# Turning decayed keys into rows of 2 KB for their way through DRAM, in a linear-attention and feed-forward kernel

## The chip, the cores and the metric

The kernel runs on one core of a Trainium2 chip. The core has TensorE (matmuls and weight loads), VectorE, ScalarE, GpSimd and SyncE, which issues most transfers, and 16 DMA engines that all queues share. The metric is the device time of one execution in microseconds; the median of several executions counts. Each engine runs its own instructions in program order, and waits on semaphores for the others.

## What is computed

Two blocks, one after the other. The first is a gated linear attention with 4 batches, 8 heads, 768 positions and head size 48; the second is a feed-forward layer of 3072 tokens, 384 to 2048 to 384, with a hard-swish between.

```python
state = np.zeros((B, H, D, D))
for t in range(S):
    state = alpha[:, :, t, :, None] * state + np.einsum('bhd,bhe->bhde', k[:, :, t], v[:, :, t])
    y[:, :, t] = np.einsum('bhd,bhde->bhe', q[:, :, t], state)
# ... (B,H,S,D) -> (B*S, H*D)
h = x @ w_in
g = h * np.clip(h + 3.0, 0.0, 6.0) / 6.0
out = g @ w_out
```

The kernel works on 24 chunks of 128 positions (6 for each batch), two chunks to a group of the feed-forward layer. In a chunk, keys and queries are scaled by running products of alpha, so that scores within the chunk are a masked matmul, and the state is carried from chunk to chunk by an update "decayed keys times values". The weights come as 64-bit floats, which the kernel rounds to 32 bits with bit operations on three engines as they arrive. From group 2 on, the feed-forward layer uses sums of blocks to save matmuls.

## The kernel before

A scheduler's freedom is switched off: the program is a list of short steps in a string, each of which calls one of these functions. The steps that matter here: `la`, `lk`, `lq`, `lv` load alpha, keys, queries and values of a chunk; `w` loads a slice of the weights, and `d1` to `d4` and `dx` round it; `z` are matmuls on an identity that keep TensorE warm; `k`, `q` scale keys and queries, `sc` are the scores, `yi` and `yx` the outputs from within and across the chunk, `u` the update of the state; `fa`, `fb`, `f` and `b` are the feed-forward layer of groups 0 and 1; `M`, `P` its products from group 2 on.

Scaled keys lie with head dimensions on the partitions (`K_t`: 128 partitions hold two heads, 64 rows each with 48 used; `NP` = 4 such pairs; 128 positions). The update needs them with positions on the partitions. For chunks 0 to 5 TensorE transposes them. From chunk 6 on VectorE turns them in blocks of 32 by 32 (`kt`), SyncE writes them to DRAM (`kw`) and reads them back so that the blocks stand in their places (`kr`). The last chunk of each batch needs no update.

```python
BLK = 32
V = C // BLK            # 4
FIRST = 6
# ...
def by_blocks(to, name, j):                  # line 292: a, k and q on their way in
    nc.vector.transpose(out=to.rearrange("r p (u v) -> r p v u", v=V),
                        in_=quads[name, j % NQ][:, :, :, 0:BLK])
# ...

    def k_in_blocks(j):
        return quads["k", j % NQ].rearrange("r p v d -> r (p v d)")[:, 0 : NP * C]

    def turn_k(j):
        to = k_in_blocks(j).rearrange("r (v p c) -> r p v c", v=V, p=NP)
        nc.vector.transpose(out=to, in_=K_t[j].rearrange("r p (v s) -> r p v s", v=V))

    def write_k(j):
        far_t[j] = far.tile([BLK, V, NP, V, BLK], FP, tag="far", name="far")
        src = k_in_blocks(j).rearrange("r (v p c) -> r (v p) c", v=V, p=NP)
        to = far_t[j].rearrange("s v p o c -> o s (v p) c")
        for o in range(V):
            nc.sync.dma_start(out=to[o], in_=src[BLK * o : BLK * (o + 1)])

    def read_k(j):
        kb_t[j] = wk.tile([C, NP, C], FP, tag="kb", name="kb")
        nc.sync.dma_start(out=kb_t[j].rearrange("s p r -> s (p r)"),
                          in_=far_t.pop(j).rearrange("s v p o c -> v s (p o c)"))
# ...
    def update(j):
        if last(j):
            return
        u = bank("u", j).rearrange("r p n -> r (p n)")[:, 0 : NP * 2 * D].rearrange(
            "r (p n) -> r p n", p=NP)
        ps_t["u", j] = u
        vs = v_t[j]
        for p in range(NP):
            for a in range(2):
                nc.tensor.matmul(u[64 * a : 64 * a + D, p, D * a : D * a + D],
                                 kb_t[j][:, p, 64 * a : 64 * a + D],
                                 vs[:, 2 * p + a, (64 - D) * a : (64 - D) * a + D],
                                 start=True, stop=True)
```

Each update is eight matmuls of which two (`a` = 0 and 1) write different halves of the partitions of one PSUM bank.

The other lines named in the text: 471 and 482 are the first matmul of the feed-forward layer in groups 0 and 1 (482 for half a group), 509 their second; 592 and 692 are the first and second product from group 2 on; 288 the transposes on TensorE; 346 the scores; 440 and 450 the outputs within and across the chunk; 524 the warming matmuls.

Of the kernel before, what the change touches and what calls it, by code (L numbers as in the profile page):

```python
# [8 lines left out]
FP = mybir.dt.float32  # L9
# [8 lines left out]
def kernel(  # L18
# [32 lines left out]
    nc = tc.nc  # L51
    B, H, S, D = q.shape
# [322 lines left out]
    def k_in_blocks(j):  # L375
        return quads["k", j % NQ].rearrange("r p v d -> r (p v d)")[:, 0 : NP * C]

    def turn_k(j):
        to = k_in_blocks(j).rearrange("r (v p c) -> r p v c", v=V, p=NP)
        nc.vector.transpose(out=to, in_=K_t[j].rearrange("r p (v s) -> r p v s", v=V))  # L380

    def write_k(j):
        far_t[j] = far.tile([BLK, V, NP, V, BLK], FP, tag="far", name="far")
        src = k_in_blocks(j).rearrange("r (v p c) -> r (v p) c", v=V, p=NP)
        to = far_t[j].rearrange("s v p o c -> o s (v p) c")
        for o in range(V):
            nc.sync.dma_start(out=to[o], in_=src[BLK * o : BLK * (o + 1)])

    def read_k(j):
        kb_t[j] = wk.tile([C, NP, C], FP, tag="kb", name="kb")  # L390
        nc.sync.dma_start(out=kb_t[j].rearrange("s p r -> s (p r)"),
                          in_=far_t.pop(j).rearrange("s v p o c -> v s (p o c)"))
# [8 lines left out]
    def update(j):  # L401
# [6 lines left out]
        for p in range(NP):  # L408
            for a in range(2):
                nc.tensor.matmul(u[64 * a : 64 * a + D, p, D * a : D * a + D],  # L410
                                 kb_t[j][:, p, 64 * a : 64 * a + D],
                                 vs[:, 2 * p + a, (64 - D) * a : (64 - D) * a + D],
                                 start=True, stop=True)
# [323 lines left out]
    with tc.manual_schedule():  # L737
        run("""la.0 z.3.5 lq.0 lk.0 lk.1 ta.0 la.1 ca.0 tq.0 r.0 lv.0.0 tk.0 lq.2 p.0 tk.1 z.0.2
            la.2 k.0 ta.1 q.0 z.0.1 lq.1 ca.1 sc.0 r.1 la.3 tq.2 z.0.5 m.0 lv.3.1 k.1 w.1 ta.2
            p.1 tq.1 ca.2 kb.0 r.2 ck.0 ta.3 u.0 ca.3 z.0.2 q.1 sm.0 sc.1 lv.1.2 p.2 la.4 kb.1  # L740
            m.1 st.1 z.0.4 ck.1 lk.2 d2.1 r.3 yi.0 w.3 d1.1 z.0.4 d3.1 cy.0 dx.1 ta.4 yi.1 q.2
            p.3 tk.2 yx.1 lk.3 k.2 d4.1 cy.1 u.1 lv.2.0 sc.2 sm.1 w.0 st.2 fa.1.0 d2.3 m.2 d1.3
            kb.2 d3.3 fb.1 ck.2 u.2 lq.3 fr.0.1 yi.2 d4.3 sm.2 w.4 fg.0.1 tk.3 st.3 f.0.3.1 k.3
            d2.0 d1.0 d3.0 ca.4 tq.3 dx.0 lq.4 r.4 yx.2 z.0.5 la.5 q.3 cy.2 d4.0 fr.0.3 sc.3
            lk.5 fg.0.3 d2.4 kb.3 m.3 w.2 d1.4 fa.0.2 dx.4 d3.4 yi.3 p.4 tk.5 yx.3 d4.4 w.5 fb.0
            cy.3 tq.4 fr.0.0 f.1.4.3 q.4 d2.2 fg.0.0 d1.2 d3.2 lq.5 dx.2 f.1.3.0 w.6 fr.1.4 d4.2
            d2.5 fg.1.4 ta.5 fa.4.1 fr.1.3 d3.5 ca.5 d1.5 w.7 f.1.2.2 r.5 fa.2.3 d2.6 fg.1.3
            d4.5 k.5 d1.6 fb.4 d3.6 w.8 f.0.5.0 fr.0.4 fr.1.2 fg.0.4 d4.6 d2.7 fg.1.2 d1.7
            f.1.5.1 d3.7 fr.0.5 w.9 fb.2 p.5 fr.1.5 d2.8 fg.1.5 d4.7 tq.5 d1.8 f.0.6.2 fg.0.5
            lk.4 q.5 fr.0.2 d3.8 w.10 ck.3 f.1.7.1 fr.0.6 fg.0.2 d2.9 d4.8 fg.0.6 d1.9 lv.4.2  # L750
            d3.9 f.0.7.0 fr.1.7 w.11 fg.1.7 d4.9 tk.4 d2.10 u.3 k.4 fr.0.7 sc.5 d3.10 d1.10
            f.1.0.3 w.12 fg.0.7 d4.10 sm.3 b.0.0.2 m.5 d2.11 st.4 fr.1.0 lv.5.0 d3.11 d1.11 w.13
            sc.4 fg.1.0 b.1.0.1 d4.11 d2.12 m.4 d1.12 d3.12 w.14 kb.4 yi.5 ck.4 d4.12 u.4
            f.1.1.0 sm.4 d2.13 st.5 d1.13 w.15 d3.13 yx.5 fr.1.1 yi.4 cy.5 fg.1.1 d2.14 f.1.6.3
            d4.13 d1.14 lk.6 d3.14 yx.4 fr.1.6 la.6 b.1.1 cy.4 fg.1.6 d4.14 d2.15 d1.15 lq.6
            d3.15 b.0.1 xc.2.1 la.7 tk.6 d4.15 b.1.2 ca.6 x.0 b.0.2 y.1 y.5 y.6 y.2 b.1.3 y.3
            y.7 y.4 y.8 y.9 b.0.3 bo.1 y.10 so.1 y.11 y.15 y.13 P.1.1.0 bo.0 s.1.0.0 so.0
            s.1.1.1 s.1.2.2 s.1.3.3 M.2.15.3 s.1.4 P.1.0.1 x.1 y.16 P.1.3.2 x.2 K.1.0 y.0 x.3
            P.1.2 K.1.2 y.17 y.12 M.2.16 y.19 K.1.1 y.18 P.1.4 y.20 y.21 xc.2.3 y.23 xc.2.4
            G.1.0 xc.2.5 O.1.0 G.1.1 M.2.0.0 xc.2.6 O.1.1 s.1.5 P.1.6 r.6 xc.2.0 k.6 P.1.5  # L760
            xc.2.7 G.1.3 kt.6 O.1.3 xc.2.8 kw.6 tq.6 xc.2.9 y.14 M.2.7.1 n.2.0.8 xc.2.2 y.22
            M.2.1 p.6 n.2.7.9 M.2.8 lv.6.1 n.2.1.10 o.2.4.0 M.2.2 q.6 e.2.4 y.24 sc.6 n.2.2.11
            xc.2.10 G.1.2 ca.7 kr.6 O.1.2 M.2.3 m.6 lk.7 M.2.18.2 M.2.4 r.7 n.2.18.12 M.2.17
            n.2.4.13 lq.7 h.2.4 M.2.19 o.2.0.0 p.7 u.6 e.2.0 M.2.9 lq.8 h.2.0 M.2.5 tk.7 yi.6
            o.2.1.0 n.2.5.14 k.7 lk.8 e.2.1 M.2.10 tq.7 cy.6 M.2.6.0 n.2.10.15 h.2.1 M.2.11 q.7
            lv.7.0 kt.7 sc.7 n.2.11.9 sm.6 kw.7 o.2.6.0 M.2.12 m.7 st.7 n.2.12.13 o.2.7.0 M.2.13
            o.2.3.0 la.8 yi.7 o.2.5.0 n.2.13.11 o.2.3.1 e.2.5 M.2.14 o.2.2.0 e.2.3 h.2.5 yx.7
            h.2.3 kr.7 P.2.0.2 cy.7 o.2.2.1 la.9 o.2.6.1 e.2.2 o.2.7.1 e.2.6 h.2.2 M.3.15.0
            h.2.6 e.2.7 xc.3.1 P.2.1.1 K.2.0 s.2.0.12 h.2.7 s.2.2.13 s.2.1.11 xc.3.3 u.7
            s.2.3.15 P.2.3.3 s.2.4 xc.3.4 tk.8 xc.3.5 G.2.0 P.2.2 xc.3.6 K.2.2 s.2.5 O.2.0  # L770
            xc.3.0 xc.3.8 xc.3.7 tq.8 M.3.0.1 K.2.1 xc.3.9 ca.8 P.2.4 n.3.0.14 xc.3.2 r.8
            xc.3.10 M.3.1 k.8 G.2.1 M.3.16 kt.8 O.2.1 n.3.1.10 p.8 kw.8 P.2.6 ca.9 q.8 r.9 M.3.2
            G.2.3 lk.9 O.2.3 M.3.7.2 sm.7 n.3.2.8 sc.8 p.9 n.3.7.9 lq.9 M.3.3 o.3.4.0 st.8 m.8
            e.3.4 M.3.8 M.3.4 h.3.4 kr.8 P.2.5 tk.9 n.3.4.11 lv.8.2 o.3.0.0 lv.9.1 k.9 e.3.0
            kt.9 la.10 M.3.9 tq.9 M.3.5 o.3.1.0 u.8 G.2.2 n.3.5.12 q.9 lk.10 M.3.18.3 O.2.2 sm.8
            e.3.1 M.3.10 h.3.0 n.3.18.13 h.3.1 M.3.6.1 n.3.10.15 kw.9 o.3.6.0 M.3.19 ca.10 st.9
            M.3.11 o.3.5.0 M.3.17 r.10 e.3.5 n.3.11.9 sc.9 lq.10 h.3.5 o.3.7.0 M.3.12 m.9 yi.8
            n.3.12.11 o.3.7.1 kr.9 M.3.13 o.3.3.0 e.3.7 la.11 yi.9 tk.10 n.3.13.8 o.3.2.0 M.3.14
            o.3.3.1 yx.9 o.3.2.1 e.3.3 h.3.7 yx.8 cy.9 h.3.3 P.3.0.3 e.3.2 s.3.1.15 cy.8 h.3.2
            s.3.3.13 o.3.6.1 P.3.1.0 xc.4.1 K.3.0 k.10 e.3.6 xc.4.3 kt.10 h.3.6 kw.10 xc.4.4 u.9  # L780
            s.3.0.11 M.4.15.1 xc.4.5 s.3.2.8 s.3.4 M.4.0.2 P.3.2 xc.4.6 n.4.0.9 lv.10.0 p.10
            lk.11 G.3.0 s.3.5 O.3.0 M.4.1 K.3.1 xc.4.0 xc.4.8 xc.4.7 P.3.4 lq.11 tq.10 n.4.1.12
# [119 lines left out]
```

## Time and profile before

| | |
|---|---|
| time, median of 3 (range) | 567.42 us (565.51 to 567.97) |
| span of the profiled execution | 564.6 us, granted TensorE clock 0.994 |
| DMA packets | 121272, 53.73 MB; 80638 of them under 512 B |
| transfers of keys to DRAM | 60 of 64 KB |
| transfers of keys back | 15 of 256 KB |
| keys turned on VectorE | 15, mean 706 ns |
| state updates | 20 blocks of 16 TensorE instructions, 11.4 us busy in all |

An fp32 matmul shows as two instructions on TensorE (PE), each with its weight load (PEld), which overlaps the matmul before it; so busy time of TensorE says that something was in the pipe, not that it ran at its best rate. The chain of waits follows the execution back from its last instruction, at each step to what released it. A group is all instructions of one line, engine and operation; "mean ns of one" is from the start of an instruction to its reported end, which for VectorE lies some 80 to 160 ns after the next one has begun. A name such as `far<-kq` is a transfer or operation that writes `far` and reads `kq`; `quads["k", ...]` is called `kq`, the far tile in DRAM `far`, the keys by position `kb`.

### The profile page before, as it was taken

Reading aid. Unit: us, or ns where it says so; the run is one execution under the profiler, and the core shown is the slowest. Engines: PE = TensorE matmul, PEld = TensorE weight load, DVE = VectorE, ACT = ScalarE, POOL = GpSimd, SP = SyncE. Lnnn points to the kernel's source line nnn. Section 1 sums busy time; section 2 is a strip of 40 time slices with the busy share of each in tenths; the row PEclk is TensorE's granted clock in tenths of the full one; section 3 lists DMA queues with packets and bytes.
Section 4 is the critical chain, followed back from the end, with each engine's and each line's share of the span. In section 5 each row is a group of like instructions: output and inputs, shape, how many; then the busy total and the mean of one; then the engine's idle time right before and its main releaser. Section 6 shows DMA issues by size and latency. Waiting matters only on the chain.

```text
span 564.6 us, 12762 instructions
## 1 busy us (share of the span) xinstructions
PE 553.4 (98%) x5236; PEld 513.2 (91%) x5236; DVE 470.0 (83%) x798; ACT 196.4 (35%) x348; POOL 56.0 (10%) x70
## 2 busy tenths in 40 slices
PE   8899999999899999999999999999999999999997
PEld 7688987599799989999999999999999999999997
DVE  7866997999899999998998978976999967754580
ACT  1457664112332332322422422432521422432420
POOL 2333435200001000100000000000000000000000
PEclk9979999999999999999999999999999999999999
DMA  9999677103533636264264353153154340000000
GB/s 147 188 186 168 186 230 196 52 16 63 139 90 87 145 71 155 54 139 90 60 148 107 77 121 85 20 146 78 45 129 94 83 122 8 1 22 8 1 30 21
DMA packets 121272, 53.73 MB, mean 95 GB/s; under 512 B 80638, under 2 KB 114174, under 8 KB 121214
## 3 DMA queue, kind: packets, MB, share of 16 engines
q1 hardware_dynamic: 114588, 48.19, 40.8%
q10 hardware_dynamic: 6624, 4.72, 2.5%
q8 instruction: 41, 0.67, 0.5%
q14 instruction: 19, 0.14, 0.1%
HBM read 44.24 MB, written 8.65 MB: 94 GB/s over the span
## 4 chain that ended last, share of the span: by engine, by line
PE 89%; DMA 6%; DVE 2%; SPq 1%; issue 0%; ACT 0%; DVEq 0%; ACTq 0%
PE m_ps L692 35%; PE m_ps L592 29%; PE m_ps L471 6%; PE sc_ps L346 4%; PE m_ps L509 4%; PE y_ps L440 4%; DMA rings<-in_k_dram 3%; PE y_ps L450 2%; PE m_ps L482 2%; DMA t<-in_v_dram 2%; PE u_ps L410 2%; DMA kb<-far 1%; PE tk_ps L288 1%; DMA far<-kq 1%; PE m_ps L524 0%
## 5 line engine op out<-in xcount | busy, mean ns | idle before, releaser
L692 PE MATMUL m_ps<-w,g_sb 128*128 128x192 f32 x704 | 121.2, 328 | 0.0
L692 PEld LDWEIGHTS m_ps<-w,g_sb 128*128 128x128 f32 x704 | 113.8, 190 | 2.3 <-issue 1.4
L598 ACT COPY g_sb<-m_ps 128x512 f32<-128x512 f32 x110 | 64.3, 584 | 138.3 <-PE m_ps L592 123.9
L692 PE MATMUL m_ps<-rings,g_sb 128*128 128x192 f32 x528 | 91.2, 326 | 0.0
L692 PEld LDWEIGHTS m_ps<-rings,g_sb 128*128 128x128 f32 x528 | 85.7, 190 | 0.0
L592 PE MATMUL m_ps<-xc,w 128*128 128x128 f32 x640 | 83.2, 278 | 0.2 <-ACT g_sb L598 0.2
L592 PEld LDWEIGHTS m_ps<-xc,w 128*128 128x128 f32 x640 | 77.2, 192 | 3.3 <-issue 1.4
L487 ACT ACTIVATE r<-g_sb,half 128x512 f32<-128x512 f32 x80 | 55.5, 719 | 57.0 <-DVE g_sb L529 22.8
L491 DVE SCALAR_TENSOR_TENSOR g_sb<-r,g_sb 128x512 f32<-128x512 f32 x80 | 54.5, 700 | 8.1 <-PE m_ps L692 4.8
L397 POOL TENSOR_TENSOR t<-t,R 128x384 f32<-128x384 f32 x20 | 20.9, 1043 | 383.8 <-DVE t L425 206.0
L592 PE MATMUL m_ps<-xT,raw 128*128 128x128 f32 x400 | 51.8, 276 | 0.0
L592 PEld LDWEIGHTS m_ps<-xT,raw 128*128 128x128 f32 x400 | 48.7, 192 | 0.3
L529 DVE TENSOR_TENSOR g_sb<-m_ps,g_sb 128x512 f32<-128x512 f32 x30 | 20.5, 686 | 27.2 <-ACT g_sb L598 26.5
L592 PE MATMUL m_ps<-xT,w 128*128 128x128 f32 x320 | 41.9, 278 | 0.0
L639 DVE TENSOR_TENSOR g_sb<-g_sb 128x512 f32<-128x512 f32 (+1 forms) x55 | 41.7, 796 | 0.1
L592 PEld LDWEIGHTS m_ps<-xT,w 128*128 128x128 f32 x320 | 38.2, 192 | 1.2 <-issue 0.2
L352 DVE TENSOR_TENSOR A<-sc_ps,mask 128x512 f32<-128x512 f32 x48 | 30.8, 683 | 2.7 <-PE sc_ps L346 2.4
L592 PE MATMUL m_ps<-xc,raw 128*128 128x128 f32 x240 | 32.1, 277 | 0.7 <-ACT g_sb L598 0.7
L471 PE MATMUL m_ps<-xT,w 128*128 128x256 f32 x144 | 32.7, 381 | 0.0
L315 DVE TENSOR_TENSOR_SCAN R<-t,ones 128x516 f32<-128x516 f32 x24 | 29.3, 1223 | 3.1 <-ACT t L306 2.8
L529 DVE TENSOR_TENSOR g_sb<-g_sb 128x512 f32<-128x512 f32 x40 | 27.2, 683 | 5.5 <-ACT g_sb L598 5.4
L592 PEld LDWEIGHTS m_ps<-xc,raw 128*128 128x128 f32 x240 | 29.9, 192 | 1.2 <-ACT g_sb L598 0.9
(110 smaller groups left out, 711.4 us busy)
## 6 DMA issues: line engine op xcount, KB each, us to landing
raw<-in_moe_w_out_dram SPq DMA_DIRECT2D x8, 768.0 KB
t<-in_v_dram SPq DMA_DIRECT2D x48, 96.0 KB
raw<-in_moe_w_in_dram SPq DMA_DIRECT2D x24, 192.0 KB
out_dram<-oh ACTq DMA_DIRECT2D x44, 96.0 KB
far<-kq SPq DMA_DIRECT2D x60, 64.0 KB
kb<-far SPq DMA_DIRECT2D x15, 256.0 KB
kq<-in_k_dram SPq DMA_DIRECT2D x36, 96.0 KB
aq<-in_alpha_dram SPq DMA_DIRECT2D x36, 96.0 KB
```

The lines of the kernel that those rows point to most:

```text
L315: nc.vector.tensor_tensor_scan(out=reverse(R, n - 1, n), data0=reverse(ax, n, n), data1=reverse(ones, n, n), initial=0.0, op0=ALU.mult, op ...
L346: nc.tensor.matmul(sc[h % 2][:, h // 2], K_t[j][r, h // 2], Q_t[j][r, h // 2], start=True, stop=True)
L352: nc.vector.tensor_tensor(out=A_t[j][:, NP * o : NP * (o + 1)], in0=ps_t.pop(("sc%d" % o, j)), in1=mask.unsqueeze(1).to_broadcast([C, NP, ...
L440: nc.tensor.matmul(y_of(j, (i + 1) // 2, p), vs[:, 2 * p + a, 32 * e : 32 * e + 32], A[:, NP * a + p], start=(i % 3 == 0), stop=(i > 1 and ...
L471: nc.tensor.matmul(h[:, f], w1[:, kk, o : o + C], xT_t[g][:, kk], start=(kk == 0), stop=(kk == KT - 1))
L487: nc.scalar.activation(out=to, in_=h, func=AF.Relu, bias=half, scale=1.0 / 6.0)
L491: nc.vector.scalar_tensor_tensor(out=to, in0=r, scalar=1.0, in1=h, op0=ALU.min, op1=ALU.mult)
L529: eng.tensor_tensor(out=out, in0=in0, in1=in1, op=ALU.add if s1 > 0 else ALU.subtract)
L592: nc.tensor.matmul(acc[g][i][:, f * C : (f + 1) * C], spots[w][:, f * C : (f + 1) * C], x_of(g, x), start=(first and f == 0), stop=last, s ...
L598: nc.scalar.copy(out=slots[z], in_=acc[g][i])
L639: nc.vector.tensor_tensor(out=out, in0=in0, in1=in1, op=ALU.subtract)
L692: nc.tensor.matmul(to[g], a, rhs[:, f], start=(first and f == 0), stop=(last and f == HF - 1), skip_group_check=True)
```

## The change

The turned keys are laid out so that the four pairs `p` are innermost: a row of the turned tile is now 512 neighbouring elements (2 KB) that go to DRAM as they lie, in one transfer of 128 rows. The way back becomes four transfers, one for each block of 32 positions, each of 32 partitions by four runs of 128 elements (512 B). In place of that, VectorE's transpose writes every fourth element, and the update reads its stationary operand with a step of four elements; it takes 64 columns instead of 48, the 16 more being rows of padding whose results nobody reads. The purpose is a shorter way for the keys through DRAM: fewer small packets, and a read that doesn't have four as its slowest dimension.

```diff
--- before.py
+++ after.py
@@ -376,20 +376,26 @@
         return quads["k", j % NQ].rearrange("r p v d -> r (p v d)")[:, 0 : NP * C]
 
     def turn_k(j):
-        to = k_in_blocks(j).rearrange("r (v p c) -> r p v c", v=V, p=NP)
+        to = k_in_blocks(j).rearrange("r (v c p) -> r p v c", v=V, p=NP)
         nc.vector.transpose(out=to, in_=K_t[j].rearrange("r p (v s) -> r p v s", v=V))
 
     def write_k(j):
-        far_t[j] = far.tile([BLK, V, NP, V, BLK], FP, tag="far", name="far")
-        src = k_in_blocks(j).rearrange("r (v p c) -> r (v p) c", v=V, p=NP)
-        to = far_t[j].rearrange("s v p o c -> o s (v p) c")
-        for o in range(V):
-            nc.sync.dma_start(out=to[o], in_=src[BLK * o : BLK * (o + 1)])
+        far_t[j] = far.tile([C, NP * C], FP, tag="far", name="far")
+        nc.sync.dma_start(out=far_t[j], in_=k_in_blocks(j))
 
     def read_k(j):
         kb_t[j] = wk.tile([C, NP, C], FP, tag="kb", name="kb")
-        nc.sync.dma_start(out=kb_t[j].rearrange("s p r -> s (p r)"),
-                          in_=far_t.pop(j).rearrange("s v p o c -> v s (p o c)"))
+        to = kb_t[j].rearrange("s p r -> s (p r)").rearrange("s (o w) -> s o w", o=V)
+        src = far_t.pop(j).rearrange("(o s) (v w) -> v s o w", s=BLK, v=V)
+        for n in range(V):
+            nc.sync.dma_start(out=to[BLK * n : BLK * (n + 1)], in_=src[n])
+
+    def k_of(j, p, a):
+
+        if j < FAR:
+            return kb_t[j][:, p, 64 * a : 64 * a + D]
+        t = kb_t[j].rearrange("s p r -> s (p r)").rearrange("s (a m p) -> s a p m", a=2, p=NP)
+        return t[:, a, p]
 
     def decayed_state(j):
 
@@ -407,8 +413,8 @@
         vs = v_t[j]
         for p in range(NP):
             for a in range(2):
-                nc.tensor.matmul(u[64 * a : 64 * a + D, p, D * a : D * a + D],
-                                 kb_t[j][:, p, 64 * a : 64 * a + D],
+                n = D if j < FAR else 64
+                nc.tensor.matmul(u[64 * a : 64 * a + n, p, D * a : D * a + D], k_of(j, p, a),
                                  vs[:, 2 * p + a, (64 - D) * a : (64 - D) * a + D],
                                  start=True, stop=True)
```

The list of steps is new as well, from the first to the last word (1649 words for 1650; the same steps, but that 29 warming matmuls stand for 28). Of both lists, the start; then, of the new one, the stretch of chunk 6:

```diff
-        run("""la.0 z.3.5 lq.0 lk.0 lk.1 ta.0 la.1 ca.0 tq.0 r.0 lv.0.0 tk.0 lq.2 p.0 tk.1 z.0.2
-            la.2 k.0 ta.1 q.0 z.0.1 lq.1 ca.1 sc.0 r.1 la.3 tq.2 z.0.5 m.0 lv.3.1 k.1 w.1 ta.2
-            p.1 tq.1 ca.2 kb.0 r.2 ck.0 ta.3 u.0 ca.3 z.0.2 q.1 sm.0 sc.1 lv.1.2 p.2 la.4 kb.1
-            m.1 st.1 z.0.4 ck.1 lk.2 d2.1 r.3 yi.0 w.3 d1.1 z.0.4 d3.1 cy.0 dx.1 ta.4 yi.1 q.2
-            p.3 tk.2 yx.1 lk.3 k.2 d4.1 cy.1 u.1 lv.2.0 sc.2 sm.1 w.0 st.2 fa.1.0 d2.3 m.2 d1.3
# ...
+        run("""lk.1 z.3.5 la.0 lk.0 la.1 tk.1 lq.0 ta.0 lv.1.0 ca.0 tk.0 r.0 la.2 ta.1 z.0.2 ca.1
+            la.3 k.0 tq.0 p.0 z.0.8 lv.0.1 r.1 lq.1 ta.2 q.0 z.0.2 ca.2 w.0 k.1 sc.0 p.1 ta.3
+            m.0 kb.0 ca.3 ck.0 tq.1 r.3 yi.0 lq.3 u.0 q.1 cy.0 w.1 p.3 sc.1 sm.0 d2.0 kb.1 m.1
+            z.0.2 st.1 ck.1 tq.3 d1.0 d3.0 u.1 lq.2 yi.1 dx.0 r.2 lk.2 yx.1 q.3 d4.0 z.1.8 cy.1
+            w.4 sm.1 d1.1 d2.1 p.2 tq.2 fa.0.0 dx.1 d3.1 tk.2 lk.3 fb.0 q.2 st.2 k.2 d4.1 lv.2.2
# ...
+            P.1.6 y.19 y.18 y.20 y.21 G.1.2 y.23 G.1.3 M.2.0.2 O.1.2 kt.6 O.1.3 M.2.7.1 n.2.0.8
+            y.24 kw.6 M.2.1 xc.2.2 n.2.7.9 p.6 M.2.8 n.2.1.10 o.2.4.0 M.2.2 q.6 e.2.4 ca.7
+            M.2.17 n.2.2.11 kr.6 sc.6 xc.2.9 tk.7 h.2.4 M.2.3 m.6 lv.7.0 M.2.4 r.7 yi.6 lq.7
+            n.2.4.12 o.2.0.0 M.2.5 cy.6 p.7 e.2.0 u.6
# ...
```

## The prediction

> **What bounds the kernel now.** I read the page first, then the waits of TensorE, then the chain of waits through the first 30 us and around chunk 6, then the groups by line and VectorE's timeline. The first part of the page:
>
> ```profile
> PE 553.4 (98%) x5236; PEld 513.2 (91%) x5236; DVE 470.0 (83%) x798; ACT 196.4 (35%) x348; POOL 56.0 (10%) x70
> ```
>
> TensorE is the bound, and it is so by more than its busy time, which says little for pipelined matmuls: the chain shows at what rate they run. In its merged pieces 16 instructions of line 692 take 2.60 us (162.5 ns each), 16 of line 592 take 1.78 us (111 ns), 32 of line 440 take 1.01 us, and these rates hold from 30 us to the end. So I can add up what TensorE has to do from the counts of the groups: 1232 of line 692 at 162.5 ns make 200.2 us; 1600 of line 592 at 111.5 ns 178.4; 144 of line 471 at 215.5 ns 31.0; 64 of line 509 at 322.5 ns 20.6; 24 score blocks of 1.09 us 26.2; 24 within-chunk blocks of 1.01 us 24.3; 20 across-chunk blocks of 0.735 us 14.7; 20 state updates of 0.495 us 9.9; 96 of line 482 at 111.5 ns 10.7; 92 transposes at 109 ns 10.0; 56 warming matmuls at 112 ns 6.3; and 60 changes from full-width to narrow matmuls, at which the last full one takes 93 ns more, 5.6. Sum 538 us of a span of 564.6. Only 26 to 27 us are lost, and no order of the same work can win more.
>
> Where they are lost: the waits of TensorE, whole span.
>
> ```profile
> PE u_ps L410 <- DMA kb<-far: 2.1, 2, 1.1
> PE tk_ps L288 <- DMA rings<-in_k_dram: 2.0, 2, 1.9
> PE m_ps L524 <- POOL ident masks.py:199: 1.5, 1, 1.5
> PE m_ps L592 <- ACT g_sb L598: 0.9, 2, 0.7
> ```
>
> Two of 15 state updates wait for the keys that come back from DRAM, together 2.1 us; the rest of any size is at the start. The chain of waits at the start (start, length, what):
>
> ```profile
> 11.86 4.27 DMA t<-in_v_dram
> 16.14 9.25 DMA rings<-in_k_dram
> 25.39 0.14 issue
> 25.53 0.64 PE tk_ps L288 x4
> ...
> 29.62 2.86 PE m_ps L482 x12
> ```
>
> The feed-forward layer begins at 29.6 us, held by the keys of chunk 2 that land at 25.4 us. The steps listed ahead of it are 18.5 us of TensorE work, so 11.1 us are lost there, 3.1 us after the last matmul (561.5 to 564.6), and the rest in short pieces.
>
> The round trip of chunk 6, in the same view:
>
> ```profile
> 132.30 0.66 DVE kq L380
> ...
> 135.09 3.06 DMA far<-kq
> 138.23 6.72 DMA kb<-far
> 145.09 0.56 PE u_ps L410 x16
> ```
>
> 12.1 us from the end of the turn (132.96) to the update; TensorE had run dry 1.1 us before.
>
> VectorE is the second bound. By windows it is busy 92 to 99% of each stretch from 100 to 300 us (49.06 of 50 us from 200 to 250), so work added there isn't free by itself. Its timeline gives the true cost of one operation, from a start to the next start:
>
> ```profile
> 132.26 0.70 DVE L380 STREAM_TRANSPOSE kq<-k 128x512 f32<-128x512 f32 x1
> 132.88 0.25 DVE L531 TENSOR_TENSOR xc<-xc,xT 128x128 f32<-128x128 f32 x1
> 133.06 1.09 DVE L292 STREAM_TRANSPOSE q<-qq 128x512 f32<-128x512 f32 x1
> 134.00 0.27 DVE L529 TENSOR_TENSOR xc<-xT,xc 128x128 f32<-128x128 f32 x1
> ```
>
> The turn of the keys (line 380, runs of 32 neighbouring elements on both sides) takes 0.62 us; the same operation writing every fourth element (line 292) takes 0.94 us.
>
> **What the skill says.** "SBUF — State Buffer", section "Door 1: The DMA port swizzle", says that SBUF has 16-byte lines and an access needs at least two hits per line for full rate. The two transposes above agree for VectorE's writes: a 16-byte step costs a factor of 1.5. No instruction of the kernel before loads weights at such a step, so for TensorE the trace is silent. "DMA: Bandwidth & Descriptors", section "Why a DMA increments its semaphore by 16 and not by 1", says that a transfer runs on the largest number of engines up to 16 that divides the slowest dimension on both sides. The old read has 4 there on the DRAM side; its 128 packets of 2 KB were in flight from 139.65 to 144.48 us, 16.3 us of packet time in 4.83 us, 3.4 engines on average, so the trace agrees. "Perfetto Trace Analysis", section "Identifying the Most-Contended Engine", takes weight-load busy time as the better measure for TensorE; 91% here, in keeping with the sum above.
>
> **Part 1, the transfers.** Before: four writes issued 0.6 to 0.7 us apart, 2048 packets of 128 B, then one read on 4 engines. From the first issue (132.99) to the read's issue 5.2 us, then 6.7. After: one write of 128 rows of 2 KB, 8 packets on each of 16 engines: 1.4 us from issue to first packet (as 138.23 to 139.65 shows), 8 x 0.13 = 1.0, 0.45 to the signal (144.48 to 144.95): 2.9 us. Four reads, 32 rows by 4 runs of 512 B, slowest dimension 32, so 16 engines: three more issues of 0.6, 1.4, about 0.4 of packets, 0.45: 4.1 us. Estimate 7.0 against 12.0. SyncE still issues five transfers. The DMA's packet time for this falls, but the DMA engines have room (busy 12 to 67% of the stretches from 100 us on). On the path this is worth the 2.1 us of waits: **-2.1**.
>
> **Part 2, the turn.** Output step of 4 elements: 0.94 instead of 0.62 us, 15 times, +4.8 us on VectorE. Four or five of them lie in the stretch where it is full, +1.3 to 1.6 us; from 320 us on VectorE has mostly 2 to 5 us of idle time in each 20. Since both engines are level there, I put a third of it on the path: **+0.5**.
>
> **Part 3, the updates.** In 15 blocks the stationary operand becomes 64 columns at a step of 16 bytes instead of 48 neighbours. Today the two matmuls for the two halves of the columns run side by side: 45 ns a pair of passes, 8 pairs and a drain, 0.495 us. Weight loads of 32, 48 and 128 columns last 107, 124 and 190 ns, about 0.87 ns a column above a fixed part. If the step is free, a load takes 64 x 0.87 = 56 ns instead of 42, the pair 58 instead of 45: 8 x 13 ns x 15 = +1.6 us. If the step costs what it costs VectorE (1.5 to 1.6), the pair takes about 90: 8 x 45 ns x 15 = +5.4 us, all on TensorE. I lean to the penalty: **+4**.
>
> **Part 4, the order.** The steps are the same but for 29 warming steps instead of 28. TensorE's sum to each milestone is nearly unchanged (227.8 against 227.6 us to the first product of group 4, 520.8 against 520.6 for group 11), and so are the full-to-narrow changes, 59 against 60. It can win only lost time. At the start, 192 KB loads with 192 B runs cost about 1.4 us each at the observed packet time (21.7 ns x 64 per engine), a 768 KB weight slice 3.3 us. Before, 14 loads and one slice, 22.8 us, give the 25.4 us of the landing. After, the feed-forward layer starts with slice 0 and waits for the queries of chunk 2, 12 loads and two slices: 23.3 us, landing at about 25.7; one transpose later it starts, at about 26.3 instead of 29.6 us, with 17.8 us of work done instead of 18.5. Gain 3.3 - 0.7 = **-2.5**. For the other short waits after 130 us (scores for queries, matmuls for evacuations, some 2 us) I count **-0.5**, and **-1.8** as trust that an order made for this kernel gains a little where I can't follow it.
>
> The slack of the updates gets smaller at the same time: TensorE's sum up to the update minus VectorE's up to the turn was 24.5 us for chunk 6 (1.1 us too short for 12.1), so a trip of 7.0 needs about 20.5; the new order has 22.6, 22.2, 25.3 and 21.4 for chunks 6, 10, 12 and 13. It uses up nearly all of the shorter trip.
>
> Sum: -2.1 + 0.5 + 4 - 2.5 - 0.5 - 1.8 = -2.4, so 567.4 becomes **565.0 us**.
>
> **Rivals.** *Weight loads as the new cost.* If 64 strided columns also lose the side-by-side run of the two halves, a pair takes 110 to 180 ns, +8 to +16 us: 573 to 580. For it: the penalty seen on VectorE. Against it: the two halves stay in separate column groups. *VectorE becomes the bound.* The new order puts more VectorE work ahead of the same products: 302.1 us by the first product of group 6 against 292.6, with TensorE at 314.5 and 312.8. The gap of about 12 us there equals the one in the stretch that was full before, so VectorE may hold TensorE up to 340 us: 568 to 571. Against it: it only fills the idle time that it had there. *The transfer was hidden anyway.* 13 of 15 updates never waited; if the start doesn't move either, there is only the dearer update: 567 to 571. *The order wins everywhere.* All of start and waits saved and free strides: about 557.
>
> **Range and chances.** The start may give 0 to 5 us, the updates cost 1.6 to 8, waits -3 to +3: 558 to 573. Over 2% faster (below 556.1) would need nearly all lost time but what the loads force: 0.04. Over 2% slower (above 578.8) needs the first rival in full or an unforeseen wait in each group: 0.06. Within: 0.90.
>
> **What would show it.** The first matmul of line 488 (482 before) near 26 us. No wait of the updates for the returning keys. The turn at 0.94 us. The update block: 0.6 us says the step is free, 0.85 the penalty, above 1.0 the first rival. VectorE at 97% up to 340 us with TensorE waiting for it says the second. I am wrong if TensorE meets waits for loads that the new order issues later, or if the read in four transfers takes longer than 6.7 us.

## The result, and the profile after

| | before | after |
|---|---|---|
| median of 4 runs each (range) | 567.25 us (565.51 to 567.97) | 572.73 us (571.64 to 573.57) |
| ratio after to before, 95% interval | | 1.0100 [1.0071, 1.0129] |
| span of the profiled execution | 564.6 us | 571.8 us |
| first matmul of the feed-forward layer | 29.55 us | 29.16 us |
| first turn of keys on VectorE begins | 132.3 us | 132.6 us |
| from there to the end of the last matmul | 429.3 us | 436.1 us |
| state update with returned keys, start to the next start | 0.495 us | 1.09 us |

The change costs 1%, 5.5 us between the medians. The table's two middle rows place it: up to the first turn the two profiles are level, and all of it lies behind, where the 15 updates with returned keys are.

The page's first part and its line of packets, kernel after:

```profile
PE 561.0 (98%) x5238; PEld 520.4 (91%) x5238; DVE 481.7 (84%) x798; ACT 196.6 (34%) x348; POOL 50.7 (9%) x70
...
DMA packets 98410, 53.73 MB, mean 94 GB/s; under 512 B 50096, under 2 KB 91312, under 8 KB 98352
```

TensorE is busy 7.6 us longer with two more instructions; VectorE 11.7 us more, 6.2 of them in the turns (15 of 1122 ns instead of 706). The transfers did what they were made for: 22862 packets fewer, 30542 fewer of them under 512 B. TensorE's waits over the whole span (us in total, times, longest):

```profile
PE y_ps L456 <- issue: 1.7, 1, 1.7
PE m_ps L530 <- POOL ident masks.py:199: 1.5, 1, 1.5
PE tq_ps L288 <- DMA rings<-in_q_dram: 1.1, 2, 0.7
PE tk_ps L288 <- DMA rings<-in_k_dram: 0.8, 2, 0.6
```

No update waits for `kb` any more; before, that was the first line of the list with 2.1 us. The price is in TensorE's timeline around chunk 6 (start, length, engine and line, operation, count). Kernel before:

```profile
145.09 0.56 PE L410 MATMUL u_ps<-t,kb 128*48 128x48 f32 x16 [1.14 <-DMA kb<-far]
145.58 1.16 PE L592 MATMUL m_ps<-xc,w 128*128 128x128 f32 x8
```

Kernel after:

```profile
141.97 1.16 PE L598 MATMUL m_ps<-xT,w 128*128 128x128 f32 x8
143.06 1.16 PE L417 MATMUL u_ps<-t,kb 128*64 128x48 f32 x16
144.15 2.05 PE L598 MATMUL m_ps<-xc,w 128*128 128x128 f32 x16
```

From 143.06 to 144.15 the update holds TensorE for 1.09 us. Thirteen of the 15 do so within 6 ns of each other, 0.597 us more than before; the other two stand next to each other in the new order and take 2.05 us together. In all it is 16.2 us instead of 7.4: **8.8 us more**. The 16 instructions of a block, called passes here, are eight pairs, in each pair one pass for each half of the partitions; the 0.597 us are 75 ns for each pair, which takes 120 ns instead of 45.

SyncE's timeline has the new round trip of chunk 6 (start and length of the issuing):

```profile
133.78 0.35 SPq L384 DMA_DIRECT2D far<-kq  x1
137.34 1.75 SPq L391 DMA_DIRECT2D kb<-far  x4
```

The keys landed at 140.6 us, 6.8 us after the first issue, and the update came at 143.06 with 2.4 us to spare. On VectorE (the same view) the turn takes from 132.59 to 133.54, 0.95 us:

```profile
132.59 1.13 DVE L380 STREAM_TRANSPOSE kq<-k 128x512 f32<-128x512 f32 x1
133.54 0.69 DVE L535 TENSOR_TENSOR w<-w 128x512 f32<-128x512 f32 x1
```

Last, TensorE's timeline at the start:

```profile
22.35 0.42 PE L456 MATMUL y_ps<-q,t 64*32 64x128 f32 x8
24.50 0.78 PE L456 MATMUL y_ps<-q,t 64*32 64x128 f32 x16 [1.72 <-issue]
25.20 3.48 PE L530 MATMUL m_ps<-ident 128*128 128x128 f32 x16
28.48 0.85 PE L288 MATMUL tq_ps<-ident,rings 128*128 128x128 f32 x4
29.16 1.50 PE L488 MATMUL m_ps<-xT,w 128*128 128x128 f32 x12
```

The queries of chunk 2 were there at 25.4 us, but ahead of their transposes in the program stand eight warming matmuls (step `z.1.8`), and these ran at half the clock: 3.3 us for 16 instructions. Ahead of them lies a wait of 1.7 us for which the profile shows no releaser. The start of the kernel before was disturbed too: in its profile the granted clock is 0.50 from 27.3 to 34.1 us.

### The profile page after: what moved, and what is told of

It reads as the page before. It is cut to its first block, busy times and chain, and to the rows that moved or that the text cites. A ratio compares the mean times of both kernels' runs of the same rounds, so it can differ in the third digit from the quotient of the medians.

```text
span 571.8 us, 12734 instructions
## 1 busy us (share of the span) xinstructions
PE 561.0 (98%) x5238; PEld 520.4 (91%) x5238; DVE 481.7 (84%) x798; ACT 196.6 (34%) x348; POOL 50.7 (9%) x70
## 4 chain that ended last, share of the span: by engine, by line
PE 88%; DVE 7%; DMA 3%; issue 1%; ACT 0%; SPq 0%; DVEq 0%
PE m_ps L698 32%; PE m_ps L598 29%; PE m_ps L477 6%; PE sc_ps L346 4%; PE y_ps L446 4%; PE m_ps L515 4%; PE u_ps L417 3%; PE y_ps L456 3%; PE m_ps L488 2%; DMA rings<-in_q_dram 1%; DVE g_sb L497 1%; PE m_ps L530 1%; DMA rings<-in_alpha_dram 1%; DVE g_sb L535 1%; DVE g_sb L645 1%
## 5 line engine op out<-in xcount | busy, mean ns | idle before, releaser
L598 PE MATMUL m_ps<-xc,w 128*128 128x128 f32 x640 | 84.4, 278 | 0.7 <-ACT g_sb L604 0.7
L493 ACT ACTIVATE r<-g_sb,half 128x512 f32<-128x512 f32 x80 | 57.6, 723 | 69.4 <-DVE g_sb L535 19.4
L403 POOL TENSOR_TENSOR t<-t,R 128x384 f32<-128x384 f32 x20 | 19.0, 950 | 393.6 <-DVE t L431 237.4
L598 PE MATMUL m_ps<-xT,w 128*128 128x128 f32 x320 | 43.1, 280 | 0.0
```

The source lines that it names most:

```text
L493: nc.scalar.activation(out=to, in_=h, func=AF.Relu, bias=half, scale=1.0 / 6.0)
L598: nc.tensor.matmul(acc[g][i][:, f * C : (f + 1) * C], spots[w][:, f * C : (f + 1) * C], x_of(g, x), start=(first and f == 0), stop=last, s ...
```

## The experiments

Each kernel was run beside the kernel before on the same chip; ratios are to that. "From the turn" is the time from the start of the first turn on VectorE to the end of the last matmul in the profile. It leaves the start out, where profiles of the same steps scatter: the first turn began between 130.0 and 133.4 us in the profiles listed here. Behind the turn, kernels that differ little in their profiles agree within 0.2 us (before and `e9`, `e5` and `e10`, after and `e1`), unless the clock dips.

The medians mix executions in which the clock was at half for some microseconds with others at full clock (granted 0.999 or more). At full clock alone the medians are 565.3 us for before (23 of its 99 executions beside the experiments), 572.4 for after (3), 571.3 for `e1` (8), 562.5 for `e4` (4), 562.0 for `e5` (5), 565.4 for `e9` (11), 562.3 for `e10` (8) and 565.0 for `e11` (12); there the change costs 7 us, as in the profiles, and not 5.5.

### The layout and the order apart

`e1_layout_only` is the changed kernel with the list of steps of the kernel before.

> The kernel after, but with the list of steps of before: transfers, turn and update are new, the order is old. Theory U (the update's 64 columns at a step of 16 bytes cost TensorE 0.60 us in each of 15 blocks, 9.0 us in all, and nothing fills them): 567.2 + 9.0 for the updates - 2.1 for the waits that the shorter trip takes away + up to 1 for the slower turn = 573 to 575, update blocks at 1.09 us. Rival O (the new order is what costs): within 2 us of before, 566 to 569.

`e2_order_only` is the kernel before with the new list of steps.

> The kernel before (old transfers, turn and update) with the new list of steps. Theory U: 572.7 - 9.0 for the updates - 1 for the turn + about 3 for updates that wait since the old trip of 12 us is longer than the new order leaves room for (after, the keys of chunk 6 landed 2.5 us ahead of their use with a trip of 6.8): 564 to 568. Rival O: 571 or more, with waits of TensorE that are not for returning keys.

Layout only: 571.95 us, ratio 1.0064 [1.0035, 1.0094], from the turn 436.3 us. It has the same updates of 1.09 us and no waits for `kb`. From the turn it is as long as the full change (436.1), so **the new order wins nothing behind the turn**. By the ratio the loss is 3.6 us (interval 2.0 to 5.3), less than the 6 to 8 expected; from the turn it is 7.0 us, as expected. This run alone doesn't say what the transfers are worth.

Order only: 578.68 us, ratio 1.0177 [1.0118, 1.0236], where 564 to 568 were expected: a miss. TensorE's waits, kernel with the new order only:

```profile
PE u_ps L410 <- DMA kb<-far: 9.3, 3, 6.4
```

One update waits 6.4 us: that of chunk 7, whose keys were turned and written at 149.9 us but whose read SyncE issued at 170.1 us. For 11.7 us of that time SyncE itself stood ahead of a load of keys, by the profile for an output transfer to land; so it was not the length of the trip alone. The clock was also at half for 13.6 us in three pieces, so not all 10 us of the ratio are waits. The new order is worse with the old transfers than with the new ones.

### What makes the update dear

Three changes of the stationary operand: fewer columns at the step of 16 bytes; 64 neighbouring columns in the kernel before; and a step of 8 bytes in the kernel before, with elements from other places, so that the right keys are left out.

```diff
 # e3_48_columns, in the changed kernel
-        return t[:, a, p]
+        return t[:, a, p, 0:D]
# ...
-                n = D if j < FAR else 64
+                n = D
 # e6_64_neighbours, in the kernel before
+                n = D if j < FAR else 64
-                                 kb_t[j][:, p, 64 * a : 64 * a + D],
+                                 kb_t[j][:, p, 64 * a : 64 * a + n],
 # e8_step_of_8_bytes, in the kernel before, from chunk 6 on
+                at = 56 * (2 * p + a)
+                keys = kb_t[j].rearrange("s p r -> s (p r)")[:, at : at + 2 * D].rearrange(
+                    "s (m t) -> s m t", t=2)[:, :, 0]
```

> The kernel after with 48 instead of 64 columns in the update, still at a step of 16 bytes. Theory S (the step makes a weight load slow, about 1.7 ns a column, and a pair of loads for the two halves still runs side by side): a pair takes 48 x 1.7 + 5 = 87 ns instead of 113, the block 0.84 to 0.89 us, the time 569 to 570. Rival W (with more than 48 columns the two halves no longer run side by side, 2 x 56 ns): a pair falls back to 45 ns, the block to 0.50 us, the time to 564.

> The kernel before with 64 neighbouring columns instead of 48 in the updates from chunk 6 on: the width alone. Theory S (the step is what is slow, 1.77 ns a column against about 0.85): a pair of passes takes 56 to 58 ns instead of 45, the block 0.58 to 0.60 us, +1.3 to 1.6 us. Were the width to break the side-by-side run, the block would take 1.03 us.

> The kernel before, with the 48 columns of each update from chunk 6 on read at a step of two elements (8 bytes) from other places of the same tile; it leaves out the right keys, so its state and output are not the reference's, and only the time counts. If what counts is two accesses for each 16-byte line, the step of 8 bytes is free: block 0.50 us. If any step costs, the block lies between 0.50 and 0.86 us, about 0.65.

The update blocks of chunk 6 in TensorE's timeline, each with the instruction after it; first 48 columns at 16 bytes:

```profile
141.68 0.93 PE L417 MATMUL u_ps<-t,kb 128*48 128x48 f32 x16
142.53 3.10 PE L598 MATMUL m_ps<-xc,w 128*128 128x128 f32 x24
```

64 neighbours:

```profile
143.64 0.67 PE L411 MATMUL u_ps<-t,kb 128*64 128x48 f32 x16 [0.89 <-DMA kb<-far]
144.24 1.16 PE L593 MATMUL m_ps<-xc,w 128*128 128x128 f32 x8
```

48 columns at 8 bytes:

```profile
145.10 0.57 PE L413 MATMUL u_ps<-t,kb 128*48 128x48 f32 x16 [1.04 <-DMA kb<-far]
145.60 1.16 PE L594 MATMUL m_ps<-xc,w 128*128 128x128 f32 x8
```

| update block, us | neighbours | step 8 B | step 16 B |
|---|---|---|---|
| 48 columns | 0.495 | 0.504 | 0.855 |
| 64 columns | 0.602 | not run | 1.09 |

The step of 16 bytes costs a factor of 1.7 to 1.8 in the block, at both widths; the width alone adds 0.11 us a block (1.6 us in 15); a step of 8 bytes is free within 0.01 us. Taken per pair as above, with what the block has beside its eight pairs held fixed, a pair takes 45 ns (48 neighbours), 58 (64 neighbours), 90 (48 columns at 16 bytes) and 120 (64 at 16 bytes): the step doubles it at both widths. The weight loads of 64 columns show it directly (count, busy time, mean ns of one); kernel after, at the step of 16 bytes:

```profile
L417 PEld LDWEIGHTS u_ps<-t,kb 128*64 128x64 f32 x240 | 15.5, 214 | 1.8 <-issue 0.4
```

64 neighbours:

```profile
L411 PEld LDWEIGHTS u_ps<-t,kb 128*64 128x64 f32 x240 | 8.3, 137 | 5.0 <-issue 2.3 <-DMA aq<-in_alpha_dram 1.8
```

With 48 columns the whole kernel takes 569.15 us, ratio 1.0014 [0.9994, 1.0034], so two fifths of what the updates grew by (0.237 of 0.597 us a block) were for rows of padding that nobody reads; that is what theory S expected for block and time. Of 64 neighbours (569.24 us) and of 8 bytes (566.93 us) there is a single time each, and only the block is used; `e6` is 4.0 us longer from the turn than before, of which 1.6 are the blocks; it also met a wait of 1.7 us for a load of alpha, with half the clock for 3.4 us after it.

Open was how: 120 ns a pair is twice the load with the halves side by side, but it is also about two loads at full rate (64 columns at 0.87 ns are 56) one after the other. `e12_halves_apart` has all first halves ahead of all second halves, in all 20 updates:

```diff
-        for p in range(NP):
-            for a in range(2):
+        for a in range(2):
+            for p in range(NP):
                 n = D if j < FAR else 64
```

> The changed kernel, but in every update the four matmuls of the first half of the partitions come first, then the four of the second, so two halves no longer alternate; the values are the same. Open is why the block of 64 columns at a step of 16 bytes takes 1.09 us: 113 ns a pair is what twice the weight load would take with the halves side by side, but also what a load at full rate (56 ns) would take twice if the halves followed one another. Theory S (dearer load, halves side by side): without the alternation the loads follow one another, and the block grows to 1.7 to 1.9 us. Rival L (full rate, the halves no longer side by side): the order of the matmuls makes no difference, 1.05 to 1.15 us. The five updates of chunks 0 to 4, with neighbouring columns, tell whether the alternation matters at all: they should go from 0.50 to 0.75 to 0.85 us.

TensorE's timeline of this kernel, the update of chunk 4, with neighbouring columns, and that of chunk 6:

```profile
86.08 0.78 PE L417 MATMUL u_ps<-t,kb 128*48 128x48 f32 x16
86.79 2.85 PE L515 MATMUL m_ps<-w,g_sb 128*128 128x384 f32 x8
...
142.04 1.68 PE L417 MATMUL u_ps<-t,kb 128*64 128x48 f32 x16
143.64 3.10 PE L598 MATMUL m_ps<-xc,w 128*128 128x128 f32 x24
```

The block grows from 1.09 to 1.60 us (under the 1.7 to 1.9 expected), that with neighbouring columns from 0.495 to 0.71 (0.75 to 0.85 expected). So the alternating halves did run side by side in the changed kernel, and rival L falls. Neither block grows to double because the halves still overlap in part: in chunk 6 the first pass of the second half starts 0.52 us after that of the first half, whose last pass starts at 0.87 us. Where one half is at work alone, a pass starts 120 ns after the one before it in chunk 6 and 45 ns in chunk 4, as the pairs do in the alternating blocks: 1.9 against 0.94 ns a column. The load itself is dear. The whole kernel took 579.72 us (a single time, beside 568.5).

### A layout with the short trip and cheap loads

`e4_runs_of_32` keeps the change's transfers and its order. The turn writes runs of 32 as before, and the update uses four narrow matmuls of 32 and 16 neighbouring columns for each pair, in four column positions, instead of two of 64 at a step.

```diff
-        to = k_in_blocks(j).rearrange("r (v c p) -> r p v c", v=V, p=NP)
+        to = k_in_blocks(j).rearrange("r (v p c) -> r p v c", v=V, p=NP)
# ...
+            for o in range(V):
+                a, n = o // 2, (BLK, D - BLK)[o % 2]
+                nc.tensor.matmul(u[BLK * o : BLK * o + n, p, D * a : D * a + D], k_of(j, p, o, n),
+                                 vs[:, 2 * p + a, (64 - D) * a : (64 - D) * a + D], ...)
```

with `k_of` cutting the run of 32 (or its first 16) at `(o p c)`.

> The kernel after with its transfers and order, but the turn writes runs of 32 neighbours (as before), and each half of an update is two matmuls of 32 and 16 neighbouring columns. Theory U with S: no step, so four narrow matmuls run side by side at about 45 to 50 ns for a pass of four, the block at 0.50 to 0.60 us, the turn at 0.62 us from start to start: 572.7 - 8 to 9 - 1 = 562 to 565. Rival W: the loads have 32 columns, so the same. Rival O: 570 or more.

`e5_runs_old_order` is the same with the list of steps of the kernel before.

> The kernel of the runs of 32 (new transfers, fast turn, four narrow matmuls) with the list of steps of before. Theory T (in the old order the transfers are worth the two waits of updates that they take away, and the order has given the rest): before - 2.1 for the waits - 0.4 for the update (0.470 instead of 0.495 us, 15 times) = 0.4 to 0.5% below before, and the new order, at 1.0% below, is worth about 3 us. Rival N (the new order gives nothing of its own; it only stands on the shorter trip): 0.8 to 1.2% below before, as the new order.

TensorE's timeline with runs of 32, chunk 6:

```profile
142.21 0.54 PE L420 MATMUL u_ps<-t,kb 128*32 128x48 f32 x32
142.68 3.14 PE L601 MATMUL m_ps<-xc,w 128*128 128x128 f32 x24
```

Twice the instructions take 0.470 us, less than the two halves took before (0.495). The Trainium skill, "TensorE: Matmul & The Clock Gate", section "Part 3: Packing small matmuls — row/col tiling", says that matmuls in different positions of the array overlap; this block agrees. The time is **562.73 us, ratio 0.9902 [0.9868, 0.9936]: faster than both kernels**. With the old order it is 562.53 us, 0.9918 [0.9889, 0.9947]; from the turn 426.7 and 426.5 us. At full clock the gain is smaller, 562.5 and 562.0 against 565.3 us. I had given the order about 3 us of its own; the rival, that it gives nothing, was right.

The same profile of `e4` shows the start as I had predicted it for the change:

```profile
23.10 0.78 PE L459 MATMUL y_ps<-q,t 64*32 64x128 f32 x16 [0.60 <-issue]
23.81 2.05 PE L533 MATMUL m_ps<-ident 128*128 128x128 f32 x16
25.70 0.60 PE L288 MATMUL tq_ps<-ident,rings 128*128 128x128 f32 x4
26.13 1.50 PE L491 MATMUL m_ps<-xT,w 128*128 128x128 f32 x12
```

The steps up to here are those of the changed kernel; only the unexplained wait is 0.6 instead of 1.7 us, the clock stays full, and the layer begins at 26.1 instead of 29.2 us. The clock is the larger part: in `e7` (below) and `e3` the same wait is 1.6 and 1.4 us, the clock stays full, and the layer begins at 27.0 and 27.3 us. With the new order it came at 26.1, 26.5, 27.0 and 27.3 us where the clock stayed full (`e4`, `e12`, `e7`, `e3`) and at 29.2 and 29.8 where it fell (after, `e2`); with the old one between 28.9 and 30.6. The gain doesn't last: in `e4` the first turn came at 131.8 us, in `e5`, whose layer began at 29.5 us, at 130.0.

### What VectorE's share costs

`e7_half_turn_twice` is `e4` with half of each turn done twice (0.37 us from start to start, 15 times, 5.5 us in all on VectorE).

```diff
+        nc.vector.transpose(out=to[:, 0 : NP // 2],
+                            in_=K_t[j][:, 0 : NP // 2].rearrange("r p (v s) -> r p v s", v=V))
         nc.vector.transpose(out=to, in_=K_t[j].rearrange("r p (v s) -> r p v s", v=V))
```

> The kernel of the runs of 32 in the new order, with the turn of two of the four pairs done a second time onto the same places: about 0.36 us more on VectorE for each of 15 chunks, 5.4 us in all, a little more than what the turn with a step cost (0.33). Theory P (the work lies mostly in VectorE's idle time): 0.5 to 2 us slower than without it, 563 to 565 or 0.6 to 0.9% below before. Rival (VectorE is the bound up to 340 us): 3 to 5 us slower, level with before or 0.3% below.

564.77 us, ratio 0.9939 [0.9918, 0.9959] where `e4` has 0.9902, 2.1 us apart on 567, with intervals that overlap; from the turn 428.4 us, 1.7 more than `e4`. By the profiles about a third of what is added to VectorE reaches the path.

### What the transfers are worth

The new transfers in the old order won more than the waits of the updates. Three more runs take that apart. `e9_keys_of_chunk_4` leaves all transfers of the kernel before as they are but lets every later update take the keys of chunk 4; `e10_extra_read` and `e11_extra_writes` give `e5` the read on four engines or the four writes of 128 B packets on top, into places that nobody uses.

```diff
 # e9, in the kernel before (kb_t[4] in a tile of its own)
-                                 kb_t[j][:, p, 64 * a : 64 * a + D],
+                                 kb_t[j if j < FAR else 4][:, p, 64 * a : 64 * a + D],
 # e10, at the end of the reading step
+        nc.sync.dma_start(out=kx, in_=f.rearrange("(v s) w -> v s w", v=V))
 # e11, at the end of the writing step
+        src = k_in_blocks(j).rearrange("r (v p c) -> r (v p) c", v=V, p=NP)
+        to = fx.rearrange("s v p o c -> o s (v p) c")
+        for o in range(V):
+            nc.sync.dma_start(out=to[o], in_=src[BLK * o : BLK * (o + 1)])
```

> The kernel before, all transfers as they are, but every state update from chunk 6 on takes the keys of chunk 4, which stay in a tile of their own, so no update waits for returning keys (the right keys are left out). The open point: the new transfers in the old order won 5.5 us, of which only 2.1 are waits of the updates. Theory W (the waits and what follows from them explain all): this kernel wins nearly as much, 4 to 5.5 us, ratio 0.990 to 0.993. Theory L (the small packets and the 4-engine read also hold up other transfers): it wins only the waits, 1.5 to 2.5 us, ratio 0.9955 to 0.9975.

> The kernel with runs of 32 in the old order, plus, after each four reads, one more read of the same 256 KB with four as its slowest dimension into a tile that nobody uses. Theory L: this read takes up to 5 us on 4 engines and holds later loads on these, so 1 to 3 us of the 5.5 come back, ratio 0.994 to 0.997. Theory W: nothing comes back, ratio 0.991 to 0.9925.

> The kernel with runs of 32 in the old order, plus, after each plain write, the four old writes (2048 packets of 128 B) into a tile in DRAM that nobody reads. Theory L: with four more issues of 0.6 us ahead of the read and the small packets, 1 to 3 us come back, ratio 0.994 to 0.998, and chunk 6's keys land about 2.5 us later. Theory W: as its updates have 2.5 us to spare, nothing or at most 0.5 us, ratio 0.991 to 0.993.

| | ratio, interval | from the turn | update of chunk 6, 10, 12: after the turn |
|---|---|---|---|
| before | 1 | 429.3 | 12.8, 90.8, 134.1 |
| e9, no update waits | 0.9985 [0.9958, 1.0012] | 429.3 | 11.6, 88.9, 134.1 |
| e11, e5 with the old writes too | 0.9985 [0.9964, 1.0006] | 428.6 | 11.6, 88.9, 133.1 |
| e10, e5 with the old read too | 0.9913 [0.9888, 0.9938] | 426.5 | |
| e5 | 0.9918 [0.9889, 0.9947] | 426.5 | 11.6, 88.4, 131.8 |

Both theories had it wrong in part. **Taking the waits of the updates away wins nothing in the end**: `e9` is ahead by 1.9 us at chunk 10 and level again at chunk 12. TensorE then waits for VectorE's and ScalarE's products in its place: 1.3 us in `e9` between these two updates, 0.2 in before. Its largest waits after 130 us in `e9`:

```profile
PE m_ps L595 <- ACT g_sb L601: 1.8, 3, 0.7
PE m_ps L595 <- DVE g_sb L536: 0.4, 1, 0.4
```

What goes with the short trip is VectorE's time: with the old transfers, or the old writes, it stands idle ahead of line 292 for keys that are loaded late. That group by line (count, busy, mean ns, idle ahead and what ended it), kernel before:

```profile
L292 DVE STREAM_TRANSPOSE k<-kq 128x512 f32<-128x512 f32 x18 | 20.1, 1115 | 5.3 <-DMA kq<-in_k_dram 5.3
```

In `e9`, the keys of chunk 4:

```profile
L292 DVE STREAM_TRANSPOSE k<-kq 128x512 f32<-128x512 f32 x18 | 20.2, 1120 | 7.0 <-DMA kq<-in_k_dram 7.0
```

In `e11`, the old writes added:

```profile
L292 DVE STREAM_TRANSPOSE k<-kq 128x512 f32<-128x512 f32 x18 | 20.1, 1116 | 7.8 <-DMA kq<-in_k_dram 7.8
```

In `e5`, the new transfers alone:

```profile
L292 DVE STREAM_TRANSPOSE k<-kq 128x512 f32<-128x512 f32 x18 | 20.0, 1109 | 0.0
```

The writes bring the idle time back, the read on four engines does not (0.0 in `e10` too). But these totals are not what is lost on the path: most of the idle time falls behind chunk 12, and from there to the end before is only 0.5 us slower than `e5`, of which about 0.25 are the dearer updates. What counts lies ahead of it. VectorE's waits for loads between 128 and 320 us, kernel before:

```profile
DVE k L292 <- DMA kq<-in_k_dram: 0.8, 1, 0.8
DVE q L292 <- DMA qq<-in_q_dram: 0.7, 1, 0.7
```

In `e9`:

```profile
DVE k L292 <- DMA kq<-in_k_dram: 2.1, 3, 0.8
```

All of these fall ahead of the update of chunk 12, by which `e5` leads both kernels by 2.3 us; `e5` and `e10` have none. In `e11` they are 1.5 us for keys and queries, and it stands 1.3 us behind `e5` there. Sizes and places agree roughly; that nothing else in the new transfers helps isn't shown.

How a load comes late shows in SyncE's timeline at chunk 15, where VectorE waits but the path doesn't depend on it; kernel before:

```profile
318.61 2.61 SPq L387 DMA_DIRECT2D far<-kq  x4
...
322.50 4.47 SPq L267 DMA_DIRECT2D kq<-in_k_dram  x4
```

and in `e5`:

```profile
313.90 0.35 SPq L384 DMA_DIRECT2D far<-kq  x1
...
315.39 1.92 SPq L267 DMA_DIRECT2D kq<-in_k_dram  x4
```

From the first write to the first load of keys SyncE needs 3.9 us with four writes, 1.5 with one; from the first to the last of the four loads it then takes 4.5 us instead of 1.9. Of these 4.5, 2.4 are no issuing: between the second load and the third (323.47 to 325.83 us) SyncE itself waits, by the profile for an output transfer. VectorE waits 1.6 us for the keys. Such waits of SyncE ahead of these loads (line 267) after 130 us, kernel before:

```profile
SPq L267 <- DMA out_dram<-oh: 27.7, 13, 4.6
SPq L267 <- DMA kb<-far: 9.0, 4, 3.1
```

In `e5`:

```profile
SPq L267 <- DMA out_dram<-oh: 7.4, 5, 2.7
```

In `e11` the first is 32.1 us, in `e10` 11.2. So the loads are late by the issuing of the writes and by SyncE's own waits; how the small packets lead to the waits wasn't tried. `e11` has one write more than the kernel before, so what it gives back (2.1 us from the turn, 0.7% or 3.8 us by the ratios) may be more than the old writes cost.

## Why the prediction held in its range and missed in its sign

The time lies just inside the range (572.7 of up to 573), but 7.7 us above the estimate and on the other side of before. That it is inside is luck: the updates cost more than the 1.6 to 8 us that the range allowed them, and the 3 us that it allowed for new waits were not needed. Two terms failed, by 4.8 us each: part 3 and part 4.

**Part 3, the updates: right mechanism, wrong size.** I wrote "I lean to the penalty: +4", between 1.6 for a free step and 5.4 for a penalty of 1.5 to 1.6. The mechanism was the penalty and it was all on TensorE; the term measured **+8.8 us**. I had taken VectorE's factor for a *whole operation* (0.94 to 0.62) as that of the weight load: 58 ns for 64 columns times 1.55 make 90 a pair. Measured it is 120, a factor of 2.1. The block of 0.85 us that I named as the mark of the penalty is exactly what 48 columns take. And leaning to a value between two cases was no estimate of either.

**The first rival had the right size for a wrong reason.** It named blocks above 1.0 us and +8 to +16 us, by two halves that no longer run side by side. The block is 1.09 us, but `e12` shows that they still do. The two hits per 16-byte line that the Trainium skill asks for ("SBUF — State Buffer", section "Door 1: The DMA port swizzle") agree with the loads on TensorE too: at a step of 8 bytes they are free, at 16 dear, by 1.7 to 1.8 in the block. The same paragraph gives 4 fp32 as how far one can stride for free; here a step of 4 is not free.

**Part 1, the transfers: amount about right, reason wrong.** The trip of chunk 6 took 6.8 us (7.0 predicted, 12.0 before) and no update waits. That this fits so well is partly luck: the write took 3.5 us instead of the predicted 2.9, the four reads 3.3 instead of 4.1. From the turn, `e5` wins 2.8 us, of which 0.4 are the cheaper updates (15 times 0.025): 2.4 against my 2.1. But `e9` shows that the 2.1 us of waits are worth nothing alone, because VectorE and ScalarE are as late; the gain comes with loads that VectorE gets sooner, which I did not see, although the idle time of 5.3 us stood in the groups. By the medians `e5` wins 5.5 us on its chip; at full clock 3.3 us (4.1 against the two such executions of before on the same chip), so a good part of what goes beyond 2.8 is the half clock that more executions of before met, and the rest stays open.

**Part 2, the turn:** 0.95 us, as predicted (0.94). Its share of the path can't be read from the change itself. By difference from the turn in `e1`, whose 15 updates stand alone and cost 9.0 us more: 436.3 − 429.3 = 7.0 = 9.0 − 2.4 + 0.4. By the slope of `e7` (1.7 of 5.5), 0.33 us times 15, or 4.95 us, would make 1.5. I had +0.5; between 0.4 and 1.5 the runs don't decide.

**Part 4, the order: the gain isn't there.** −2.5 at the start, −0.5 for short waits and −1.8 of trust did not come. Behind the turn the order makes no difference (after against `e1`, `e4` against `e5`). At the start the prediction of 26.3 us came true to 0.2 us in `e4`, and not in the profile of the change (29.2). I had overlooked the eight warming matmuls behind the wait, which cost 1.9 us at full clock and 3.3 at half; in `e4` too they, and not the queries (there at 25.45 us), are what the transposes at 25.70 follow. I took a start that varies by 3 us between profiles of the same steps for a fixed one, and read the clock in neither: before was at half from 27.3 us on, which makes up 1.1 of the 11.1 us that I counted as lost. Nor does an early layer last to the first turn (131.8 us in `e4`, 130.0 in `e5`). By the ratios the order is worth 0 within the intervals.

**Sum:** −2.4 for the transfers, +0.4 to 1.5 for the turn, +8.8 for the updates, 0 for the order make 6.8 to 7.9 us. The interval of the ratio is 4.0 to 7.3, the two profiles are 7.2 apart, 6.8 of it from the turn. The 0.4 was itself taken from a difference of profiles, so the sum shows less than it seems to.

**The other rivals.** VectorE as the bound up to 340 us: the windows show it busy 48.1 to 49.3 of each 50 us from 100 to 250, but TensorE stays at 49.3 to 50, so it did not become the bound in the change; in `e9`, where no update waits, TensorE waits 1.8 us for ScalarE's products and 0.9 for VectorE's. The transfer hidden anyway, 567 to 571: nearly the time, and nearer the truth than I gave it, since the waits were worth nothing; but the transfers did win.

## What to carry to other kernels

A layout that saves packets can be paid for by whoever reads it last: before a stationary operand gets a step of 16 bytes, look for a cut into narrower matmuls of neighbouring columns, which here took no longer than two wide ones and kept the gain of the transfers. A wait that ends last on the busiest engine is worth its length only if the next engine is not as late itself; take the wait alone away to see it. The idle time of an engine counts only where the path depends on it: of VectorE's 5.3 us for keys, 4.5 fell where it did not. Look for the cost of many small writes not at their reader but at the loads that stand behind them in the same queue.

## What the runs showed of the hardware

- A step of two fp32 elements in the stationary operand is free (0.504 against 0.495 us a block), a step of four is not: 0.855 against 0.495 us for 48 columns, 1.09 against 0.602 for 64, which is twice the time for each pair of passes.
- The clock fell to half for 3.4 us after a wait of only 1.7 us, in the midst of a start with several waits (after) or behind a single one (`e6` at 222.8 us). The Trainium skill's "TensorE: Matmul & The Clock Gate", section "HAM oscillation — how this bites in real kernels", speaks of gaps above about 3.4 us; these were shorter. The length of one wait doesn't decide it here: waits of 1.7 us in `e1` and 2.7 in `e5`, both at the start, left the clock at full. The window from 24.9 to 29 us, kernel after (busy time and instructions of the five engines, then granted clock, DMA share and GB/s):

```profile
24.90:29.00 4.10, 4.10 (x30) 3.90 (x28) 2.62 (x3) 3.66 (x5) 1.87 (x2) 0.58 0.99 220
```

The same window of `e4`:

```profile
24.90:29.00 4.10, 4.10 (x39) 4.10 (x38) 3.00 (x5) 3.56 (x3) 1.82 (x2) 1.00 0.72 190
```

TensorE is busy throughout in both, but at a clock of 0.58 it gets through 30 instructions instead of 39.
- One plain write of 256 KB took 0.35 us to issue; the four of 64 KB with 128 B runs took 2.6 us at chunk 15, 3.5 at chunk 6.
